# Full-row score products, normalization of attention moved behind the output product, and a new order of the fillers

## The chip, the cores and the metric

The kernel runs on one core of a Trainium2 chip. The metric is the device time of one execution in microseconds (us). TensorE is called PE in the rows, VectorE DVE, ScalarE ACT, GpSimd POOL and SyncE SP; SP issues nearly all DMAs.

## The reference

Three layers follow each other on 8 batches of 576 positions: a retention layer with 8 heads of 64, a mixture of 4 attention experts of which each token takes 2, and a layer with a rotation by sine and cosine and a mixing over positions. Cut to what matters here:

```python
# retention
scores = (1/8) * q @ k.T;  ret = scores * decay;  x = ret @ v          # [8, 576, 512]
# experts e = 0..3, head size 64
logits = x @ w_gate;  topk, w = best 2 of 4, softmax over the two
q, k, v = x @ wq[e], x @ wk[e], x @ wv[e]
s = (1/8) * q @ k.T, causal;  a = exp(s - max);  a /= a.sum() + 1e-9
out[token] += w[token, e] * (a @ v @ wo[e])                              # where e is in topk
# last layer
theta = out @ w_theta;  zr, zi = out*cos(theta), out*sin(theta)
u = out + w_tok_r @ zr + w_tok_i @ zi;  result = u + relu(u @ w_ch)
```

The division by the sum and the gate's weight w scale each row of a, so they may also be applied to the rows of a @ v.

## The kernel before

Products that need more than one pass of precision split a number into a high part h and a low part l: `split` (L91) writes h on ACT and l = x - h on DVE, and `mm3` (L86) adds three matmuls.

The first half of the program runs over 80 attention units (b, p, m): batch b, pair p of two experts (s = 0, 1), and block m of 128 query rows (64 in the last, m = 4). The loop at L535 does one unit's scores, then the transposes of the unit before, and the output product when a group of blocks is complete (groups are m = 0; 1 and 2; 3 and 4). Between these it calls `fill`, which takes pieces of other work from a list: projections of the second pair of this batch, then retention, V and the projections of the next batch. How much is taken is set by a table of costs, `COST` for the units and one number per piece, and `FO`. The program is then put in order by a scheduler for each engine, so the rows of an engine do not stand in the order of the code.

For a pair, `proj_qk` (L184) makes U, which holds for each expert the high part of q in one half of the partitions and its low part in the other half, and K. K's high part KN is copied by four DMAs on SP into both halves of KK (L200); K's low part KL stays where it is.

`at_scores` (L260) multiplies U by KK over all 128 rows (L272), so that high and low part of q meet the high part of K in one matmul, and then adds, over 64 rows only, the high part of q by KL (L275). On DVE L278 adds the causal mask and finds the row minimum of the negated scores, on ACT L283 takes the exponential and its row sum. `at_norm` (L287) then divides the gate's weight by the sum on three small DVE instructions (L292 to L294) and scales the row block, on DVE for s = 0 (L297) and on ACT for s = 1 (L299). `at_trans` (L310) transposes the block on PE (L324) and copies it to PT, on DVE for s = 0 and on ACT for s = 1 (L329, L331). `at_out` (L333) multiplies V by PT (L343), and ACT copies the result to ob (L347), which goes out to a DRAM tile OD. Scores, transposes and outputs share four PSUM tiles named a.

The second half reads OD back (`load_o`, L477, tiles ol) and makes token tiles from it (`token_tile`, L481); nine of them are made early, in the last batch of the first half. Then follow `mix` (L621) and `channel` (L671), whose result POOL completes (L684).

Of the kernel before, what the change touches and what calls it, by code (L numbers as in the profile page):

```python
# [9 lines left out]
F32 = mybir.dt.float32  # L10
# [34 lines left out]
FO = 0.5  # L45
NDVE = (0,)
# [7 lines left out]
def tile_kernel(ctx: ExitStack, tc: tile.TileContext, qk, kv, w1, wo, wot, wd, cst, out):  # L54
# [10 lines left out]
    TT = [dram.tile([128, 2, DM], F32, name=f"tt{k}") for k in range(4)]  # L65
    att = pool("att", side="right")
# [9 lines left out]
    LG = [att.tile([128, NCH, E], F32, name=f"lg{i}") for i in range(2)]  # L76
    WH = w1p.tile([128, 4, NW1], F32R, name="WH")
# [106 lines left out]
    def proj_qk(b, p, t, g):  # L184
        xh, xl = XT[b]
        if (b, p) not in QKP:
            QKP[b, p] = (att.tile([128, 2, S], F32R, name="U", bufs=2), att.tile([128, 2, S], F32R, name="KK", bufs=2),
                         att.tile([128, S], F32R, name="KL", bufs=2), att.tile([128, S], F32R, name="KN", bufs=1))
        U, KK, KL, KN = QKP[b, p]
# [5 lines left out]
        if t:  # L195
            split(KN[:, sl], KL[:, sl], ps)
            if g:
                for s in range(2):
                    for o in range(2):
                        nc.sync.dma_start(KK[o * 64:o * 64 + 64, s, :].bitcast(F32),  # L200
                                          KN[s * 64:s * 64 + 64, :].bitcast(F32))
            return
# [57 lines left out]
    def at_scores(u):  # L260
        b, p, m = u
        U, KK, KL, _ = QKP[b, p]
# [3 lines left out]
        st = att.tile([128, 4, 2], F32, name="st", bufs=3)  # L266
        parts = [(0, n)] if n <= 512 else [(0, HS), (HS, S)]
        Ps = [att.tile([128, S], F32, name="P", bufs=PB_N) for _ in range(2)]
        for i, (j0, j1) in enumerate(parts):
            ps = [ps1.tile([128, j1 - j0], F32, name="a", bufs=AB, padded_shape=[128, 512]) for _ in range(2)]  # L270
            for s in range(2):
                nc.tensor.matmul(ps[s][:R], U[:, s, rs], KK[:, s, j0:j1], start=True, stop=False)  # L272
            for s in range(2):
                hs = slice(s * 64, s * 64 + 64)
                nc.tensor.matmul(ps[s][:R], U[hs, s, rs], KL[hs, j0:j1], start=False, stop=True)  # L275
# [6 lines left out]
        for s in range(2):  # L282
            MARK["act"] = nc.scalar.activation(Ps[s][:R, :n], Ps[s][:R, :n], AF.Exp, bias=st[:R, last, s:s + 1], scale=-1.0,  # L283
                                 accum_out=st[:R, 2, s:s + 1])
        PB[u] = (Ps, st)

    def at_norm(u):  # L287
        b, p, m = u
        Ps, st = PB[u]
        R = ROWS[m]  # L290
        n = min(C * (m + 1), S)
        nc.vector.tensor_scalar(st[:R, 3, :], st[:R, 2, :], 1e-9, None, op0=OP.add)  # L292
        nc.vector.reciprocal(st[:R, 3, :], st[:R, 3, :])
        nc.vector.tensor_mul(st[:R, 3, :], GW[b][:R, m, 2 * p:2 * p + 2], st[:R, 3, :])  # L294
        for s in range(2):
            if s in NDVE:
# [494 lines left out]
```

## Time and profile before

| | us |
|---|---|
| median of 3 runs | 986.61 (985.03 to 989.39) |
| the profiled execution | 989.46 |
| span of its instructions | 987.7 |
| PE busy in the span | 958.8 |
| DVE, ACT, POOL busy | 683.4, 487.1, 226.7 |

An engine's busy time is the union of its instructions' times. Matmuls are pipelined: one starts before the one ahead has ended, so the time that a matmul costs is read from the distance between starts. A wait is idle time of an engine, put down to what ended it.

### The profile page before, as it was taken

Reading aid. Unit: us, or ns where it says so; the run is one execution under the profiler, and the core shown is the slowest. Engines: PE = TensorE matmul, PEld = TensorE weight load, DVE = VectorE, ACT = ScalarE, POOL = GpSimd, SP = SyncE. Lnnn points to the kernel's source line nnn. Section 1 sums busy time; section 2 is a strip of 40 time slices with the busy share of each in tenths; the row PEclk is TensorE's granted clock in tenths of the full one; section 3 lists DMA queues with packets and bytes.
Section 4 is the critical chain, followed back from the end, with each engine's and each line's share of the span. In section 5 each row is a group of like instructions: output and inputs, shape, how many; then the busy total and the mean of one; then the engine's idle time right before and its main releaser. Section 6 shows DMA issues by size and latency. Waiting matters only on the chain.

```text
span 987.7 us, 21586 instructions
## 1 busy us (share of the span) xinstructions
PE 958.8 (97%) x8090; PEld 848.1 (86%) x8090; DVE 683.4 (69%) x2099; ACT 487.1 (49%) x1278; POOL 226.7 (23%) x278
## 2 busy tenths in 40 slices
PE   6999999999999999999999999999999999999998
PEld 6988878778787877777767899999999999999998
DVE  5498887888978779687576783485655746486533
ACT  2366656656666565566567652344333432344320
POOL 4334262452624525332000001020200102020110
PEclk9999999999999999999999999999999999999999
DMA  9755563654635636354631301010001001010001
GB/s 267 199 166 155 154 194 89 195 172 124 212 111 171 194 106 204 98 163 132 243 127 37 121 2 48 14 60 25 36 13 37 37 1 49 1 38 12 25 26 48
DMA packets 64185, 101.45 MB, mean 103 GB/s; under 512 B 15184, under 2 KB 37072, under 8 KB 64080
## 3 DMA queue, kind: packets, MB, share of 16 engines
q1 hardware_dynamic: 63936, 99.79, 33.1%
q8 instruction: 64, 1.05, 0.4%
q0 software_dynamic: 144, 0.28, 0.1%
q14 instruction: 41, 0.34, 0.1%
HBM read 67.22 MB, written 23.66 MB: 92 GB/s over the span
## 4 chain that ended last, share of the span: by engine, by line
PE 83%; DVE 10%; DMA 3%; issue 1%; ACT 1%; SPq 1%; POOL 1%; ACTq 0%; POOLq 0%
PE acc L658 24%; PE w L87 12%; PE w L88 11%; PE w L89 11%; PE a L343 4%; PE a L324 4%; PE a L272 3%; PE a L275 2%; PE w L125 2%; PE w L157 2%; PE w L153 2%; PE acc L648 2%; DMA kv<-kv 2%; DVE P L278 2%; DVE sm L130 1%
## 5 line engine op out<-in xcount | busy, mean ns | idle before, releaser
L658 PE MATMUL acc<-TK,zh 128*128 128x256 f32 (+1 forms) x1024 | 183.8, 302 | 0.0
L658 PEld LDWEIGHTS acc<-TK,zh 128*128 128x128 f32 x1024 | 152.4, 190 | 0.7 <-DVE ul L93 0.2
L684 POOL TENSOR_TENSOR o<-o,ul 128x576 f32<-128x576 f32 x28 | 41.9, 1500 | 435.2 <-DVE o L679 435.2
L283 ACT ACTIVATE P<-P,st 128x128 f32<-128x128 f32 (+4 forms) x160 | 95.8, 599 | 69.4 <-DVE st L278 68.6
L658 PE MATMUL acc<-TK,zl 128*128 128x256 f32 (+1 forms) x512 | 110.0, 297 | 0.0
L278 DVE CUSTOM_DVE_ANT_0 P<-a,cm 128x128 f32<-128x128 f32 (+4 forms) x160 | 72.8, 476 | 26.9 <-PE a L275 26.4
L658 PEld LDWEIGHTS acc<-TK,zl 128*128 128x128 f32 x512 | 86.2, 189 | 0.1
L602 ACT ACTIVATE cs<-cs 128x512 f32<-128x512 f32 x72 | 45.2, 630 | 80.3 <-DVE cs L600 76.7
L92 ACT ACTIVATE zh<-cs 128x512 fp32r<-128x512 f32 x64 | 40.2, 630 | 81.3 <-PE acc L658 67.0
L87 PE MATMUL w<-xh,WH 128*128 128x288 f32 x256 | 79.9, 312 | 0.0
L93 DVE TENSOR_TENSOR zl<-cs,zh 128x512 fp32r<-128x512 f32 x64 | 45.0, 707 | 50.4 <-ACT zh L92 49.4
L88 PE MATMUL w<-xl,WH 128*128 128x288 f32 x256 | 76.3, 298 | 0.0
L324 PE MATMUL a<-ident,P 128*128 128x128 f32 (+2 forms) x480 | 65.2, 265 | 11.1 <-DVE P L297 5.2
L87 PE MATMUL w<-uh,CH 128*128 128x256 f32 (+1 forms) x256 | 75.8, 296 | 0.0
L89 PE MATMUL w<-uh,CH 128*128 128x256 f32 (+1 forms) x256 | 75.8, 296 | 0.0
L88 PE MATMUL w<-ul,CH 128*128 128x256 f32 (+1 forms) x256 | 75.8, 296 | 0.0
L89 PE MATMUL w<-xh,WL 128*128 128x288 f32 x256 | 75.6, 295 | 0.0
L604 DVE SCALAR_TENSOR_TENSOR cs<-cs,x 128x512 f32<-128x512 f32 x72 | 55.4, 775 | 24.6 <-ACT cs L602 24.5
L125 PE MATMUL w<-qz,kt 128*64 128x256 f32 (+1 forms) x576 | 61.8, 334 | 7.7 <-DMA kt<-qk 5.1
L167 POOL TENSOR_TENSOR xl<-xt,xh 128x512 fp32r<-128x512 f32 (+1 forms) x40 | 50.7, 1269 | 78.8 <-ACT xh L166 78.8
L324 PEld LDWEIGHTS a<-ident,P 128*128 128x128 f32 (+2 forms) x480 | 45.7, 138 | 26.1 <-DVE P L297 7.4
L93 DVE TENSOR_TENSOR ul<-acc,uh 128x256 fp32r<-128x256 f32 x64 | 25.7, 450 | 59.3 <-ACT uh L92 59.1
(141 smaller groups left out, 2484.7 us busy)
## 6 DMA issues: line engine op xcount, KB each, us to landing
kv<-kv SPq DMA_DIRECT2D x40, 512.0 KB, 4.8
KK<-KN SPq DMA_DIRECT2D x64, 144.0 KB, 2.5
raw<-wd SPq DMA_DIRECT2D x43, 192.0 KB, 2.8
qz<-qk SPq DMA_DIRECT2D x64, 128.0 KB, 4.1
kt<-qk SPq DMA_DIRECT2D x32, 256.0 KB, 3.7
out<-o SPq DMA_DIRECT2D x28, 288.0 KB, 2.1
td<-hl SPq DMA_DIRECT2D x27, 192.0 KB, 2.5
TK<-td SPq DMA_DIRECT2D x9, 576.0 KB, 8.0
```

The source lines that it names most:

```text
L87: nc.tensor.matmul(ps, ah, bh, start=first, stop=False)
L88: nc.tensor.matmul(ps, ah, bl, start=False, stop=False)
L89: nc.tensor.matmul(ps, al, bh, start=False, stop=last)
L93: nc.vector.tensor_sub(l, src, h)
L125: nc.tensor.matmul(ps[e][g, i, :, j * 64:R], t[:, hp, j * 64:j * 64 + 64], qz[:, :, hp, j * 64:R], start=True, stop=True, skip_group_check ...
L167: nc.gpsimd.tensor_sub(xl[:, :, cs], xt, xh[:, :, cs])
L278: MARK["dve"] = nc.vector.tensor_tensor_reduce(Ps[s][:R, j0:j1], ps[s][:R], cm[:R, o + j0:o + j1], 1.0, st[:R, 0, s:s + 1] if i else 3.0e3 ...
L283: MARK["act"] = nc.scalar.activation(Ps[s][:R, :n], Ps[s][:R, :n], AF.Exp, bias=st[:R, last, s:s + 1], scale=-1.0, accum_out=st[:R, 2, s:s ...
L324: nc.tensor.transpose(tp[:w, j, :], Ps[s][:R, j * C:j * C + w], ident[:R, :R])
L602: nc.scalar.activation(cs, cs, AF.Sin)
L604: nc.vector.scalar_tensor_tensor(z, cs, -1.0, x2[:, None, ds].to_broadcast([128, 2, 256]), op0=OP.mult, op1=OP.mult)
L658: nc.tensor.matmul(acc[d][j], A[:, dc], TK[:, kt, W, t0:t1], start=q == 0 and n == 0, stop=q == 8 and n == 2)
```

## The change

Both parts of K are now split into one tile KN of two parts (two buffers instead of one), and the four DMAs copy both into KK, so that the low product also runs over 128 rows with the same U; it now adds low part by low part as well. The sums of the exponentials are kept for a whole pair in SUM. `at_norm` runs once per pair: it makes the quotients for all five blocks, transposes them on DVE in squares of 32, and four DMAs write them as rows to a DRAM tile GD. `load_o` reads them back, spread over 64 partitions by four DMAs, and POOL multiplies ol by them. In the loop, part of the fillers now comes before the transposes and the rest after them; `COST` and `FO` have other numbers.

```diff
-FO = 0.5
-NDVE = (0,)
+FO = 0.45
...
+    GD = [dram.tile([2, 2, 640], F32, name=f"gd{b}") for b in range(B)]
...
+    SUM = [att.tile([128, NCH, 2], F32, name=f"sum{i}") for i in range(2)]
+    NW = [att.tile([128, 32], F32, name=f"nw{i}") for i in range(2)]
...
-            QKP[b, p] = (att.tile([128, 2, S], F32R, name="U", bufs=2), att.tile([128, 2, S], F32R, name="KK", bufs=2),
-                         att.tile([128, S], F32R, name="KL", bufs=2), att.tile([128, S], F32R, name="KN", bufs=1))
+            QKP[b, p] = (att.tile([128, 2, S], F32R, name="U", bufs=2), att.tile([128, 2, 2, S], F32R, name="KK", bufs=2),
+                         att.tile([128, 2, S], F32R, name="KN", bufs=2))
...
-            split(KN[:, sl], KL[:, sl], ps)
+            split(KN[:, 0, sl], KN[:, 1, sl], ps)
...
-                        nc.sync.dma_start(KK[o * 64:o * 64 + 64, s, :].bitcast(F32),
-                                          KN[s * 64:s * 64 + 64, :].bitcast(F32))
+                        nc.sync.dma_start(KK[o * 64:o * 64 + 64, s, :, :].bitcast(F32),
+                                          KN[s * 64:s * 64 + 64, :, :].bitcast(F32))
...
             for s in range(2):
-                nc.tensor.matmul(ps[s][:R], U[:, s, rs], KK[:, s, j0:j1], start=True, stop=False)
-            for s in range(2):
-                hs = slice(s * 64, s * 64 + 64)
-                nc.tensor.matmul(ps[s][:R], U[hs, s, rs], KL[hs, j0:j1], start=False, stop=True)
+                for x in range(2):
+                    nc.tensor.matmul(ps[s][:R], U[:, s, rs], KK[:, s, x, j0:j1], start=x == 0, stop=x == 1)
...
-                                 accum_out=st[:R, 2, s:s + 1])
+                                 accum_out=SUM[p][:R, m, s:s + 1])
...
+        x = SUM[p]
+        w = NW[p][:, :2 * NCH].rearrange("q (m s) -> q m s", m=NCH)
-        nc.vector.tensor_scalar(st[:R, 3, :], st[:R, 2, :], 1e-9, None, op0=OP.add)
-        nc.vector.reciprocal(st[:R, 3, :], st[:R, 3, :])
-        nc.vector.tensor_mul(st[:R, 3, :], GW[b][:R, m, 2 * p:2 * p + 2], st[:R, 3, :])
-        for s in range(2):
-            if s in NDVE:
-                nc.vector.tensor_scalar(Ps[s][:R, :n], Ps[s][:R, :n], st[:R, 3, s:s + 1], None, op0=OP.mult)
-            else:
-                nc.scalar.activation(Ps[s][:R, :n], Ps[s][:R, :n], AF.Copy, scale=st[:R, 3, s:s + 1])
+        nc.vector.tensor_scalar(w, x, 1e-9, None, op0=OP.add)
+        nc.vector.reciprocal(w, w)
+        nc.vector.tensor_mul(w, GW[b][:, :, 2 * p:2 * p + 2], w)
+        wt = att.tile([128, 32], F32, name="nwt", bufs=2)
+        nc.vector.transpose(wt, NW[p])
+        for a in range(4):
+            nc.sync.dma_start(GD[b][p].rearrange("s (m a q) -> a m s q", m=NCH, a=4)[a], wt[a * 32:a * 32 + 2 * NCH, :])
...
     def load_o(b):
         OL[b] = wk1.tile([128, 2, S], F32, name="ol", bufs=3)
         nc.sync.dma_start(OL[b], OD[b])
+        gw = wk1.tile([128, 2, S], F32, name="og", bufs=1)
+        for s in range(2):
+            for p in range(2):
+                nc.sync.dma_start(gw[s * 64:s * 64 + 64, p, :], GD[b][p, s, :S].partition_broadcast(64))
+        nc.gpsimd.tensor_mul(OL[b], OL[b], gw)
...
-    COST = [0.7, 1.1, 1.6, 2.2, 2.2]
+    COST = [0.9, 1.2, 1.7, 2.2, 2.4]
...
+        goal = tot * (k + 1) / 10 if t < nu else 1e9
+        fill(done + FO * max(goal - done, 0.0), k)
         if t >= 1:
             at_trans(units[t - 1])
-        goal = tot * (k + 1) / 10 if t < nu else 1e9
-        fill(goal - FO, k)
+            if units[t - 1][2] == NCH - 1:
+                at_norm(*units[t - 1][:2])
+        fill(goal, k)
         if t >= 1:
             ub, up, um = units[t - 1]
             if GROUPS[GRP[um]][-1] == um:
                 at_out(ub, up, GRP[um])
-        if t < nu:
-            at_norm(units[t])
-        fill(goal, k)
```

The scheduler makes of this another order. The first place is on PE, in the second batch, from the transposes of block 2 to the scores of block 4. P is transposed by ident (128x128), V by PT is the output product, U by KK and KL the scores, and qz, kt, sm, S and vp belong to retention; the line of dots stands for the two rows ahead of it once more. Before:

```order
L324 MATMUL a<-ident,P 128x128 x6
L153 MATMUL w<-qz_111,S_108 64x128
L157 MATMUL w<-sm_114,vp 64x128 x2
L157 MATMUL w<-sm_115,vp 64x128 x2
...
L343 MATMUL a<-PT,V 64x256 x4
L343 MATMUL a<-PT,V 64x128 x2
L272 MATMUL a<-KK,U 64x288 x2
L275 MATMUL a<-KL,U 64x288 x2
L272 MATMUL a<-KK,U 64x288 x2
L275 MATMUL a<-KL,U 64x288 x2
```

The same place on PE now, where L322 transposes, L341 makes the output and L127 belongs to retention:

```order
L322 MATMUL a<-ident,P 128x128 x6
L127 MATMUL w<-qz_122,kt 64x256 x2
L127 MATMUL w<-qz_122,kt 64x2x64
L341 MATMUL a<-PT,V 64x256 x4
L341 MATMUL a<-PT,V 64x128 x2
L275 MATMUL a<-KK,U 64x288 x8
L322 MATMUL a<-ident,P 128x128 x8
```

The four steps between high and low part are one row of eight equal matmuls, and three products instead of nine stand between the transposes and the output that reads their copies.

The second place is on PE at the border between two batches, where the first scores of the new pair (128 columns) stand among the projections of the other pair (xh, xl by WH, WL). Before:

```order
L89 MATMUL w<-xh,WL 128x288
L87 MATMUL w<-xh,WH 128x288
L272 MATMUL a<-KK,U 128x128
L275 MATMUL a<-KL,U 128x128
L272 MATMUL a<-KK,U 128x128
L275 MATMUL a<-KL,U 128x128
L324 MATMUL a<-ident,P 128x64 x4
L324 MATMUL a<-ident,P 64x64
```

The same border on PE now; the line of dots stands for 21 projections:

```order
L89 MATMUL w<-xh,WH 128x288
L90 MATMUL w<-xl,WH 128x288
L275 MATMUL a<-KK,U 128x128 x2
L91 MATMUL w<-xh,WL 128x288
L89 MATMUL w<-xh,WH 128x288
...
L89 MATMUL w<-xh,WH 128x288
L275 MATMUL a<-KK,U 128x128 x2
L322 MATMUL a<-ident,P 128x64 x4
L322 MATMUL a<-ident,P 64x64
```

The scores of the second expert have moved behind almost two more projections.

The third place is on SP, where the second half's inputs are first read back. Before:

```order
L200 DMA KK<-KN 64x576 x2
L479 DMA ol<-od_60 128x1152
L479 DMA ol<-od_61 128x1152
L479 DMA ol<-od_62 128x1152
L349 DMA od_67<-ob 128x576
L479 DMA ol<-od_63 128x1152
```

The same place on SP now; gd are the quotients, og their spread copy, nwt the transposed quotients:

```order
L479 DMA ol<-od_60 128x1152
L483 DMA og<-gd_85 64x576 x4
L479 DMA ol<-od_61 128x1152
L297 DMA gd_92<-nwt 5x2x32 x3
L483 DMA og<-gd_86 64x576 x4
L297 DMA gd_92<-nwt 5x2x32
L347 DMA od_67<-ob 128x576
```

Each read of ol is followed by four reads of quotients, and the quotients of the last batch are written between them.

## Rows read from the trace of the kernel before

**Rows 1.** The page's first part: busy us (share of the span) and instructions

```profile
PE 958.8 (97%) x8090; PEld 848.1 (86%) x8090; DVE 683.4 (69%) x2099; ACT 487.1 (49%) x1278; POOL 226.7 (23%) x278
```

**Rows 2.** Stretches: length, busy PE, PEld, DVE, ACT, POOL, clock, DMA, GB/s

```profile
40.00:560.00 520.00, 504.15 (x4755) 413.35 (x4754) 411.87 (x1482) 322.52 (x947) 166.73 (x221) 0.99 0.50 152
120.00:160.00 40.00, 38.60 (x418) 31.72 (x414) 32.05 (x115) 24.36 (x75) 17.77 (x22) 0.96 0.54 164
200.00:240.00 40.00, 38.47 (x347) 33.36 (x345) 30.83 (x109) 23.71 (x77) 16.86 (x24) 0.96 0.46 128
320.00:360.00 40.00, 37.85 (x369) 32.77 (x367) 30.28 (x118) 24.73 (x79) 19.03 (x25) 0.96 0.50 149
```

**Rows 3.** Waits of PE: us in total, times, the longest one

```profile
PE a L324 <- DVE P L297: 5.2, 7, 1.4
PE a L324 <- DVE st L278: 2.9, 4, 1.3
PE a L324 <- ACT ob L347: 2.8, 2, 1.5
PE w L87 <- ACT oh L92: 1.3, 1, 1.3
```

**Rows 4.** Timeline of PE, scores of 256 columns: start, us, then the instruction

```profile
204.31 0.50 PE L272 MATMUL a<-KK,U 128*128 128x256 f32 x2
204.74 0.38 PE L275 MATMUL a<-KL,U 64*128 64x256 f32 x2
205.06 0.33 PE L324 MATMUL a<-ident,P 128*128 128x128 f32 x1
```

**Rows 5.** Timeline of PE, scores of 384 columns

```profile
213.24 0.52 PE L272 MATMUL a<-KK,U 128*128 128x384 f32 x2
213.69 0.45 PE L275 MATMUL a<-KL,U 64*128 64x384 f32 x2
214.06 0.33 PE L324 MATMUL a<-ident,P 128*128 128x128 f32 x1
```

**Rows 6.** Timeline of PE, scores of twice 288 columns, the first half

```profile
225.29 0.29 PE L89 MATMUL w<-xh,WL 128*128 128x288 f32 x1
225.42 0.43 PE L272 MATMUL a<-KK,U 128*64 128x288 f32 x2
225.78 0.35 PE L275 MATMUL a<-KL,U 64*64 64x288 f32 x2
226.06 0.34 PE L272 MATMUL a<-KK,U 128*64 128x288 f32 x1
```

**Rows 7.** Timeline of PE, scores of 128 columns at a batch border

```profile
231.43 0.22 PE L272 MATMUL a<-KK,U 128*128 128x128 f32 x1
231.58 0.32 PE L275 MATMUL a<-KL,U 64*128 64x128 f32 x1
231.84 0.33 PE L272 MATMUL a<-KK,U 128*128 128x128 f32 x1
```

**Rows 8.** Timeline, eight transposes and the copy of the second four on ACT

```profile
227.24 1.03 PE L324 MATMUL a<-ident,P 128*128 128x128 f32 x8
...
229.28 0.57 ACT L329 COPY PT<-a 128x512 f32<-128x512 f32 x1
```

**Rows 9.** Groups by line: instructions, then busy us, mean ns, idle before

```profile
L299 ACT ACTIVATE P<-P,st 128x128 f32<-128x128 f32 (+4 forms) x80 | 48.3, 604 | 15.5 <-DVE st L294 14.3
...
L684 POOL TENSOR_TENSOR o<-o,ul 128x576 f32<-128x576 f32 x28 | 41.9, 1500 | 435.2 <-DVE o L679 435.2
L297 DVE TENSOR_SCALAR P<-P,st 128x128 f32<-128x128 f32 (+4 forms) x80 | 40.8, 510 | 1.5
...
L294 DVE TENSOR_TENSOR st<-gw,st 128x2 f32<-128x2 f32 (+1 forms) x80 | 18.1, 226 | 0.8
```

**Rows 10.** DMAs of KK (the page's sixth part) and of ol (time to landing)

```profile
KK<-KN SPq DMA_DIRECT2D x64, 144.0 KB, 2.5
...
DMA to landing us min/median/max: 3.4/4.4/6.4
```

More of the change, by code (lines that the diff above doesn't have):

```diff
@@ L186, in proj_qk @@
         if (b, p) not in QKP:
-            QKP[b, p] = (att.tile([128, 2, S], F32R, name="U", bufs=2), att.tile([128, 2, S], F32R, name="KK", bufs=2),
-                         att.tile([128, S], F32R, name="KL", bufs=2), att.tile([128, S], F32R, name="KN", bufs=1))
-        U, KK, KL, KN = QKP[b, p]
+            QKP[b, p] = (att.tile([128, 2, S], F32R, name="U", bufs=2), att.tile([128, 2, 2, S], F32R, name="KK", bufs=2),
+                         att.tile([128, 2, S], F32R, name="KN", bufs=2))
+        U, KK, KN = QKP[b, p]
         w0 = (2 * p + t) * 128
@@ L261, in at_scores @@
         b, p, m = u
-        U, KK, KL, _ = QKP[b, p]
+        U, KK, _ = QKP[b, p]
         R = ROWS[m]
@@ L265, in at_scores @@
         rs = slice(m * C, m * C + R)
-        st = att.tile([128, 4, 2], F32, name="st", bufs=3)
+        st = att.tile([128, 2, 2], F32, name="st", bufs=3)
         parts = [(0, n)] if n <= 512 else [(0, HS), (HS, S)]
@@ L283, in at_scores, with at_norm @@
             MARK["act"] = nc.scalar.activation(Ps[s][:R, :n], Ps[s][:R, :n], AF.Exp, bias=st[:R, last, s:s + 1], scale=-1.0,
-                                 accum_out=st[:R, 2, s:s + 1])
[L285 to L291, printed above, removed]
-        nc.vector.tensor_scalar(st[:R, 3, :], st[:R, 2, :], 1e-9, None, op0=OP.add)
-        nc.vector.reciprocal(st[:R, 3, :], st[:R, 3, :])
-        nc.vector.tensor_mul(st[:R, 3, :], GW[b][:R, m, 2 * p:2 * p + 2], st[:R, 3, :])
-        for s in range(2):
-            if s in NDVE:
-                nc.vector.tensor_scalar(Ps[s][:R, :n], Ps[s][:R, :n], st[:R, 3, s:s + 1], None, op0=OP.mult)
-            else:
-                nc.scalar.activation(Ps[s][:R, :n], Ps[s][:R, :n], AF.Copy, scale=st[:R, 3, s:s + 1])
+                                 accum_out=SUM[p][:R, m, s:s + 1])
+        PB[u] = Ps
+    def at_norm(b, p):
+        x = SUM[p]
[7 more added lines that the diff above has]
+            nc.sync.dma_start(GD[b][p].rearrange("s (m a q) -> a m s q", m=NCH, a=4)[a], wt[a * 32:a * 32 + 2 * NCH, :])
     def pt_view(PT, g, j):
@@ L311, in at_trans @@
         b, p, m = u
-        Ps, _ = PB.pop(u)
+        Ps = PB.pop(u)
         R = ROWS[m]
@@ L366, in tile_kernel @@
         nc.gpsimd.memset(l, 0.0)
+    for x in SUM + NW:
+        nc.gpsimd.memset(x, 1.0)
     loads(0, 0)
```

## The prediction

> **What bounds the kernel now.** Read the busy line first [rows 1]: PE is busy for 958.8 of 987.7 us, DVE for 683.4, ACT for 487.1. So only two things can move the time: work that leaves or joins TensorE's own stream, and the moments in which that stream stands still. Then cut the span into stretches [rows 2]. In 40 to 560 us, where attention, retention and projections run, PE is busy for 504.15 of 520 us, so it idles 15.9 us, while DVE is busy for 79% and ACT for 62% of it. Three stretches of 40 us have a mean granted clock of 0.96, which is a mixture of the two levels 2.4 and 1.2 GHz; each loses 0.04 x 40 = 1.6 us, and in each PE had idled for 1.4 to 2.2 us. All that the change does to the order lies before 560 us; behind that it adds only work for POOL and the DMA queues.
>
> The table of waits says who holds PE up [rows 3]: transposes that wait for the normalization on DVE (5.2 us), for the row minima (2.9) and for a PSUM tile that ACT still copies from (2.8), and a token tile that waits for the split of its input (1.3). Last come the single matmuls around a score [rows 4 to 7]. L272 is the full-row product with K's high part, L275 the 64-row product with its low part. What I read there is not how long one takes but how far its start lies from the next start.
>
> **Term 1, the scores on PE.** The number of matmuls stays (192 + 192 become 384), only their rows change. A full-row matmul of 288 columns is followed by the next after 225.42 - 225.29 = 0.13 us [rows 6]; in proportion to columns I estimate 0.12 for 256, 0.175 for 384 and 0.235 for 512. For 128 columns the same rule gives 0.06; the eight transposes of 128 columns took 1.03 us, 0.13 each at most and 0.11 if the last one's tail is taken off [rows 8]. I take 0.11 and keep 0.06 and 0.13 as ends.
> At 384 columns, two L272 occupy 0.45 us up to the first L275, and the two L275 0.37 up to the next instruction [rows 5]. Four full rows would take 4 x 0.175 = 0.70, so 0.12 goes. The first pair alone should take 0.35; the 0.10 more is the price of entering the 64-row products. The pair of L275 takes no less than two full ones (0.37 against 0.35), though both share a time slot. At 288 columns it is 0.36 and 0.28 = 0.64 against 0.52 [rows 6]: 0.12, twice in a unit of the last rows. At 256 columns 0.75 [rows 4], of which some 0.09 is the entry from the 64-column products ahead, which stays: against 0.48 + 0.09 it is 0.18. At 512 I estimate 0.10 + 0.47 + 0.43 against 0.94: 0.06. At 128 columns one single L272 with its L275 takes 231.84 - 231.43 = 0.41 [rows 7] against 2 x 0.11: 0.19. Eight of the sixteen units of 128 columns are cut in this way, s by s, as in the second place of the section on the change, and save 0.38 each; the other eight save an estimated 0.14.
> Sum: (0.12 + 0.24 + 0.18 + 0.06) x 16 = 9.6, and 8 x 0.38 + 8 x 0.14 = 4.2: 13.8 us, with the ends of the 128-column spacing 12.5 to 16.2. The order has about as many changes between 128- and 64-column products as before, so these cancel. Term 1: -14.
> Here a page of the Trainium skill speaks against the change. Both matmuls of an L275 pair lie on different row halves, and the rows show that the pair takes 0.28 us at 288 columns [rows 6], where two in a row at 0.13 would take 0.26 without any entry or exit. The Trainium skill, "TensorE: Matmul & The Clock Gate", Part 3 (packing small matmuls), says that matmuls on different row groups run concurrently, so that packing them gains. By that rule, unpacking adds one streaming per pair; the rows bear it out for the pair but show more lost at its edges, so the sum goes by the rows.
>
> **Term 2, the normalization leaves the units.** Per unit three small DVE instructions (the last 226 ns), one scaling on DVE (510 ns) and one on ACT (604 ns) go; 80 of each, 40.8 us on DVE and 48.3 on ACT for the scalings, 18.1 for one of the three small ones [rows 9]. In their place come, once per pair, three small ones and a transpose, 64 instead of 400. None of that was PE's work, so it counts only by PE's waits. The wait for L297 (5.2) has no cause any more. Of the two others (2.9 and 2.8), I take half, since minima and output copies remain while DVE and ACT have less in front of them: -2.9. Together -8. With the waits, two of the three stretches at 0.96 should return to full clock: 2 x 1.6 = -3.2. The ends: nothing of this, or all 15.9 us of idling and 4.8 of clock.
>
> **What it adds.** (a) K's parts: a pair's four DMAs carry twice the bytes, and the first waits for DVE's low part as well as ACT's high part. The row has 2.5 us to landing for the present size [rows 10]; more bytes lie between 2.5 and 5. At the eight batch borders the order now puts the second head's 128-column score behind two more projections' worth of work, some 3 us, so the later landing is covered; if not, each border costs up to 1 us. I take 1 us in all, ends 0 and 8. (b) The output product now stands closer behind its transposes. By the order, 19 of 48 outputs have less than 1.3 us of PE's work after their last transpose, 6 before. The copies in between are on DVE and ACT: in the rows ACT's copy began 1.0 us and ended 1.6 us after the eight transposes [rows 8], because exponentials stood ahead of it. In the new order half of the fillers lie between score and transpose, so ACT should be through with them. I take 0.1 us at each of the 19 places, 2 us. (c) 64 small DMAs on SP for the quotients, in groups of four that wait for the transpose on DVE; behind them stand loads that are needed much later, so nothing. (d) In the second half eight POOL products of 1152 columns: from 1500 ns for 576 columns [rows 9] 3.0 us each, plus 32 DMAs of the size of a KK transfer. POOL is nearly empty there. Only the first token tile can feel it: its input lands after 4.4 us [rows 10] and PE already waits 1.3 us for it; now four more DMAs and 3 us of POOL come on top. But the order has moved that tile two scores later, some 4 us of PE's work. I take 0.5 us, ends -1.3 and +5.
> Sum: -14 - 8 - 3.2 + 1 + 2 + 0.5 = -21.7. From the profiled execution's own 989.46 us that is 967.8. This execution was 2.85 us above the median of 986.61, as I guess by waits or slow-clock stretches of the kind that I remove, so part of the gain is already in the median: between 964.9 and 967.8 I forecast 967.
>
> **The rivals.** (B) Only PE's own stream gets shorter: the waits that go are replaced by others of the same size. For it: each of them is a single wait below 2 us, and every reordering makes new ones. Against: DVE's work in that stretch falls from 411.87 us by 40.8, by some 50 for the small ones, and gains some 15, which leaves about 68% of a shorter stretch. 986.6 - 14 + 1 = 974. (C) The pairs' concurrency was worth what the page says and their edges cost nothing that leaves: then each pair of batch and head pair adds 0.06 + 0.12 + 0.175 + 0.235 + 2 x 0.13 = 0.85 us, 16 times 13.6, against 9 from the waits: 991. Against it stand the 0.45 and 0.37 [rows 5]. (D), on the other side: outputs wait for late copies. If ACT's copy still ends 1.6 us behind the transposes, 19 outputs wait up to 1.2 us each, 23 us, and half a dozen more stretches fall to 0.96 for 1.6 us each, 10: 986.6 - 14 - 8 + 33 = 998. It decides against the gain as soon as the mean wait at those places passes 1 us. For it: the copy row. Against: the exponentials now end earlier, and DVE's copies are prompt. (E) The first token tile waits for its weighted input: 5 us and a stretch of slow clock, 974.
>
> **How the numbers follow.** Forecast 0.70 (own range 958 to 977), B 0.12, C 0.05, D 0.08, E 0.05. The lowest end is -16.2 - 15.9 - 4.8 with nothing added, about 951; the highest within the forecast's mechanism is -12.5 with 13 of additions, about 986. The range that leaves out two in ten is 954 to 984. Within 0.5%, 981.7 to 991.5, a measurement of this kernel can't tell from no change. Faster by more takes nearly all of the forecast and E and most of B: 0.84; within it are most of C and rests of B and D: 0.08; slower: 0.08.
>
> **What would show it.** Right: scores whose starts follow each other at 0.12 to 0.24 us with no step before the second half of a pair; PE busy for some 490 us before a boundary that lies near 540; no wait for a scaled P; no or one stretch at 0.96. Wrong: output products at PE's head that wait for PT copies (D), scores that wait for KK's landing, a token tile that waits for POOL (E), or score groups that last longer than now (C).

## The result, and the profile after

The changed kernel takes 998.7 us (median of 4 runs, 994.8 to 1002.0), the kernel before in the same comparison 985.8 (984.7 to 989.4). The ratio is 1.0122, with a 95% interval of 1.009 to 1.0154: slower by 1.2%, clear of the noise, where 967 us were forecast with a range of 954 to 984.

The busy line of the page after, beside [rows 1]: PE is busy for 6 us less and the span has grown by 12.

```profile
PE 952.8 (95%) x8090; PEld 863.1 (86%) x8090; DVE 647.5 (65%) x1843; ACT 445.7 (45%) x1198; POOL 244.5 (24%) x290
```

The stretches of after, columns as in [rows 2], with one more from the end of the first half:

```profile
40.00:560.00 520.00, 487.64 (x4699) 418.48 (x4698) 360.54 (x1207) 275.02 (x854) 172.26 (x225) 0.97 0.60 172
...
200.00:240.00 40.00, 35.02 (x293) 31.58 (x287) 23.13 (x79) 17.84 (x60) 14.65 (x20) 0.87 0.48 134
520.00:560.00 40.00, 34.16 (x179) 25.43 (x179) 22.81 (x57) 19.69 (x49) 8.51 (x4) 0.96 0.40 118
```

ACT is emptier as worked out (275.0 us instead of 322.5) and DVE less so (360.5 instead of 411.9, where the prediction's sum for rival B comes to some 336). And yet PE stands still for 32 of 520 us instead of 16. The mean clock of the stretch has gone from 0.99 to 0.97, that of 200 to 240 us from 0.96 to 0.87.

The waits of PE after. No row of [rows 3] is left among the large ones; the first is new, and as large as all the waits on DVE before:

```profile
PE a L341 <- DVE PT L327: 14.9, 13, 3.6
PE w L127 <- DMA kt<-qk: 7.0, 4, 2.8
PE pS L89 <- DVE nr L513: 3.5, 2, 2.3
PE a L341 <- ACT PT L327: 3.0, 3, 1.4
PE w L89 <- DVE nr L513: 2.8, 3, 2.1
PE a L275 <- DMA KK<-KN: 2.5, 2, 1.3
PE acc L663 <- DVE zl L95: 1.8, 1, 1.8
```

L341 is the output product and L327 the copy of the transposed P (PT) out of PSUM: output products wait 17.9 us, at 16 places, for PT copies. The L127 row, retention's load, was there before (5.1 us).

To compare kernels I cut each span of a trace into three: **idle** (between PE's first and last instruction neither PE nor its weight loads run), **clock** (half of the time in which 1.2 GHz instead of 2.4 were granted, that is the span times one minus the mean granted clock) and the rest, PE's **stream**, which includes some 5 us ahead of PE's first instruction and behind its last.

| us | span | idle | clock | stream |
|---|---|---|---|---|
| before | 987.7 | 23.6 | 8.5 | 955.6 |
| after | 1000.0 | 41.8 | 18.8 | 939.5 |
| difference | +12.3 | +18.2 | +10.3 | -16.1 |

So the gain that was forecast in the stream came, and more than all of it was handed back in waits and in the slow clock that follows them. The table has one execution of each kernel, and that of after is the slowest of four. Over all executions with a recorded clock the clock's part is 9.9 to 19.0 us in after (median 14.0, n = 4) and 2.9 to 12.9 before (median 5.9, n = 25): the difference is nearer to 8 us than to 10.3, and the clock column of a single trace is uncertain by several us.

**What the late copy waits for.** The longest wait of after, 3.60 us, as a timeline of PE, DVE and POOL:

```profile
206.50 3.24 PE L341 MATMUL a<-PT,V 128*64 128x192 f32 x20 [3.60 <-DVE PT L327]
...
202.84 0.26 DVE L410 TENSOR_SCALAR ex<-raw 128x192 int32<-128x192 int32 x1 [2.05 <-POOL r L416]
203.02 0.74 DVE L408 SCALAR_TENSOR_TENSOR b<-raw,b 128x192 int32<-128x192 int32 x1
203.80 1.30 DVE L412 SCALAR_TENSOR_TENSOR b<-ex,b 128x192 f32<-128x192 int32 x1
...
205.42 0.69 DVE L166 TENSOR_TENSOR xt<-w,gt 128x512 f32<-128x512 f32 x1
206.03 0.41 DVE L327 COPY PT<-a 128x256 f32<-128x256 f32 x1
...
201.21 1.04 POOL L113 TENSOR_TENSOR vp<-kv,gam 128x512 f32<-128x512 f32 x1 [2.23 <-DMA kv<-kv]
202.21 0.59 POOL L416 TENSOR_TENSOR r<-r,ex 128x192 f32<-128x192 f32 x1
```

The transposes were through at 202.2. The PT copy (L327) began at 206.03, since in the trace DVE runs in the order of its queue, and ahead of the copy stood a weight conversion (L407 to L413, the jobs that the loop spreads over the first half) and retention's product xt (L166). Its second step waited 2.05 us for POOL, which held the only buffer ex and had itself waited 2.23 us for retention's kv. In the trace of before 4 of DVE's 112 PT copies have a conversion instruction between the last score reduction and themselves, 4 instructions in all; in after 48 copies have 145. The product xt stands between a last reduction and its copy 42 times in after and never before.

Conversions are late for their own loads too. In the trace of before neither DVE nor ACT has a wait for loaded words (raw); after:

```profile
ACT r L415 <- DMA raw<-wd: 13.6, 10, 3.4
DVE b L407 <- DMA raw<-wd: 11.8, 8, 2.6
```

From the issue of such a load on SP to the moment when DVE is free for it pass 12.1 us before (median of 51) and 5.9 after. A possible reason stands in SP's own queue (the fourth round tests it), where L297 is now the store of the quotients (64 pieces of 1.2 KB; ns min/median/max):

```profile
L297 SPq DMA_DIRECT2D gd<-nwt x64: 686/732/1270, 78.4 to 552.1; - x64
```

Each takes SP 0.73 us to issue, longer than a load of words (L400, most of them 192 KB: median 0.43 in after, 0.34 before). The lengths of all of SP's DMA issues between 40 and 490 us sum to 169 us before and to 238 after; of the 69 more, these stores are 39 and the doubled key parts 13.

### The profile page after: what moved, and what is told of

It reads as the page before. It is cut to its first block, busy times and chain, and to the rows that moved or that the text cites. A ratio compares the mean times of both kernels' runs of the same rounds, so it can differ in the third digit from the quotient of the medians.

```text
span 1000.0 us, 21417 instructions
## 1 busy us (share of the span) xinstructions
PE 952.8 (95%) x8090; PEld 863.1 (86%) x8090; DVE 647.5 (65%) x1843; ACT 445.7 (45%) x1198; POOL 244.5 (24%) x290
## 4 chain that ended last, share of the span: by engine, by line
PE 74%; DVE 9%; DMA 6%; ACT 2%; issue 2%; SPq 1%; POOL 0%; DVEq 0%; ACTq 0%; POOLq 0%
PE acc L663 23%; PE w L89 9%; PE w L90 9%; PE w L91 9%; PE a L341 5%; PE a L275 5%; PE w L127 3%; PE a L322 3%; DMA raw<-wd 3%; PE acc L653 2%; PE w L159 2%; DMA KK<-KN 1%; DVE P L278 1%; PE w L155 1%; DVE b L412 1%
## 5 line engine op out<-in xcount | busy, mean ns | idle before, releaser
L275 PE MATMUL a<-KK,U 128*64 128x288 f32 (+4 forms) x384 | 81.0, 335 | 4.6 <-DMA KK<-KN 2.5
L341 PE MATMUL a<-PT,V 128*64 128x192 f32 (+3 forms) x576 | 66.6, 351 | 18.1 <-DVE PT L327 14.9
L89 PE MATMUL w<-xh,WH 128*128 128x288 f32 x256 | 77.7, 304 | 0.0
L341 PEld LDWEIGHTS a<-PT,V 128*64 128x64 f32 (+1 forms) x576 | 41.7, 147 | 39.9 <-DVE PT L327 17.7
L609 DVE SCALAR_TENSOR_TENSOR cs<-cs,x 128x512 f32<-128x512 f32 x72 | 59.7, 835 | 24.6 <-ACT cs L607 24.5
L275 PEld LDWEIGHTS a<-KK,U 128*128 128x128 f32 (+1 forms) x384 | 57.1, 178 | 17.1 <-issue 5.6
L169 POOL TENSOR_TENSOR xl<-xt,xh 128x512 fp32r<-128x512 f32 (+1 forms) x40 | 47.1, 1178 | 86.7 <-ACT xh L168 85.5
```

The lines of the kernel that those rows point to most:

```text
L89: nc.tensor.matmul(ps, ah, bh, start=first, stop=False)
L169: nc.gpsimd.tensor_sub(xl[:, :, cs], xt, xh[:, :, cs])
L275: nc.tensor.matmul(ps[s][:R], U[:, s, rs], KK[:, s, x, j0:j1], start=x == 0, stop=x == 1)
L341: nc.tensor.matmul(po[s * 64:s * 64 + 64, c0:], V[:ROWS[j], j, 2 * p + s, :], v, start=j == 0, stop=j == last, skip_group_check=True)
L609: nc.vector.scalar_tensor_tensor(z, cs, -1.0, x2[:, None, ds].to_broadcast([128, 2, 256]), op0=OP.mult, op1=OP.mult)
```

## The experiments

**First round: the parts one at a time.** Rows alone put the four full-row matmuls of a score into the kernel before; normalization alone moved only that; order alone took only the loop, FO and COST; and the last kept all of the change but gave it the old loop, FO and COST.

```diff
 # order alone; e4 is the reverse of it on the changed kernel
-FO = 0.5
+FO = 0.45
-    COST = [0.7, 1.1, 1.6, 2.2, 2.2]
+    COST = [0.9, 1.2, 1.7, 2.2, 2.4]
+        fill(done + FO * max(goal - done, 0.0), k)
         at_trans(units[t - 1])
-        fill(goal - FO, k)
+        fill(goal, k)
         at_out(ub, up, GRP[um])
...
```

> The kernel before with the full-row scores alone (both parts of K in KK, larger KK transfers); normalization and loop order as before. Theory 1 (the new order of transposes, fillers and outputs costs the time): the score stream is 13 to 16 us shorter and little of it is lost to waits, so 0.983 to 0.988 of before. Theory 2 (more and larger DMAs on SP delay the conversion's loads, and DVE stands behind them): part of it is lost again, 0.990 to 1.000. Theory 3 (PE's time is given by waits that any shorter stream refills): 0.995 to 1.005.

> The kernel before with the normalization moved to the second half alone (quotients transposed on DVE, written by small DMAs, read back and multiplied on POOL); scores and loop order as before. Theory 1: the waits for the scaled P go, 5 us, so 0.990 to 0.998, less up to 4 us where POOL's products hold DVE up. Theory 2: the 64 small DMAs on SP delay the loads behind them, PT copies wait on DVE, 1.000 to 1.010. Theory 3: 0.995 to 1.005.

> The kernel before with the new loop order and cost table alone (part of the fillers before the transposes, the normalization of each unit after the output). Theory 1: output products wait for PT copies as in the changed kernel, 1.010 to 1.030. Theory 2: without the added DMAs the copies come in time, 0.995 to 1.005. Theory 3: 0.995 to 1.005.

> The changed kernel with the loop order and cost table of before: full-row scores and the moved normalization, transposes directly behind the scores, then fillers, then the output. Theory 1: both gains show, 0.975 to 0.985. Theory 2: as slow as the changed kernel, 1.005 to 1.015. Theory 3: 0.995 to 1.005.

| | ratio (95%) | idle | clock | stream |
|---|---|---|---|---|
| e1, rows alone | 1.0029 (1.0004 to 1.0055) | 32.2 | 8.5 | 946.5 |
| e2, normalization alone | 1.0019 (0.9999 to 1.0039) | 27.1 | 8.5 | 947.9 |
| e3, order alone | 1.0213 (1.0179 to 1.0248) | 35.7 | 17.9 | 951.7 |
| e4, all but the order | 1.0015 (0.9983 to 1.0047) | 37.0 | 10.2 | 938.4 |

The loss is the order's: alone it costs 2.1%, and under it rows and normalization together gain 0.9%. (Theory 1 fits e3, theory 3 fits e1 and e4, and e2 lies where theories 2 and 3 overlap.) The first wait of e3 is the one of after:

```profile
PE a L343 <- DVE PT L329: 15.0, 8, 3.3
```

Yet no engine waits for loaded words in e3. In the longest of these waits (3.31 us, up to 146.05) DVE worked all the time: from 142.40 us on, when a wait for POOL had ended, it ran a conversion, the three small instructions of the normalization, a scaling of P and xt ahead of the copy. So the new order loses time at the copies also where every load is in time.

But the order is not the whole story. In e1 and e4 the stream is 9 and 17 us shorter and the time is not. In e1 (first fence) the waits of [rows 3] have grown to fill it; in e4 (second) the copies of outputs on ACT (ob) and PT copies are late:

```profile
PE a L322 <- DVE P L295: 8.4, 14, 1.9
PE a L322 <- ACT ob L345: 7.2, 5, 3.0
```

```profile
PE a L322 <- ACT ob L345: 10.3, 6, 2.5
PE a L341 <- DVE PT L327: 6.4, 7, 2.0
...
ACT r L415 <- DMA raw<-wd: 13.2, 8, 3.4
DVE b L407 <- DMA raw<-wd: 12.1, 9, 2.6
```

**Second round: what stands ahead of the copies.**

```diff
 # e5: a job is issued behind the latest PT copy of its engine
+            MARK["dve" if s in PTV else "act"] = copy(PT[...], tp[...])
 # e6, e7: more buffers for the conversions
-raw bufs=2, b1/ex/r/d bufs=1, hl bufs=2
+raw bufs=4, b1/ex/r/d bufs=2, hl bufs=3
 # e8
-FO = 0.45
+FO = 0.0
```

> The changed kernel with one thing moved: each conversion job is issued behind the latest PT copy of DVE and of ACT instead of behind the latest reduction and exponential of a score, which takes conversion instructions out of the way of many PT copies (in the trace of the changed kernel 48 of DVE's 112 copies have 145 conversion instructions between the last score reduction and themselves; of the kernel before 4 have 4). Theory 1 (head of line: outputs wait because the in-order queues of DVE and ACT hold a conversion job, itself late for its load or for POOL, ahead of a PT copy): TensorE's waits for PT copies fall from 18 us to 7 or less, the slow-clock loss from 15 to 9, so the ratio to the kernel before comes to 0.995 (0.988 to 1.002). Theory 2 (distance: outputs stand too close behind the transposes, whatever is ahead in the queues): the waits for PT copies stay at 15 or more and the ratio at 1.012 (1.008 to 1.016).

> The changed kernel with more buffers for the conversions (4 instead of 2 for the loaded words, 2 instead of 1 for each intermediate, 3 instead of 2 for the result), the order of the scores, transposes and outputs nearly as before. Theory 1 (head of line, and the job is late because its load is): DVE's and ACT's waits for the loaded words, 11.8 and 13.6 us, fall below 5 each, TensorE's waits for PT copies from 18 to 11, the ratio from 1.012 to 1.003 (0.996 to 1.008). Theory 2 (distance): the waits for loaded words fall, but those for PT copies stay at 15 or more, ratio 1.012. If the loads come no earlier with more buffers because SP's queue holds them, both numbers stay.

> Full-row scores and the moved normalization under the old order, with more buffers for the conversions (as in the run beside it). Under the old order without them the ratio was 1.0015, with 12.1 and 13.2 us of waits on DVE and ACT for the loaded words and 28 us of TensorE's idling. Theory 1 (late conversion jobs hold copies up): idling falls to 20 us, slow clock to 8.5, ratio 0.991 (0.984 to 0.997). Theory 2 (the copies themselves and their distance): the waits for loaded words go but the ratio stays at 1.001 (0.998 to 1.005).

> The changed kernel with the share of fillers between a score and the transposes of the unit before it set from 0.45 to 0, so that all of them stand between transposes and output; the cost table is the new one. Theory 2 (distance) says: TensorE's waits for PT copies fall from 18 to some 7 us, as under the old order, and transposes that wait for exponentials or for a PSUM tile take 6 to 10 in their place; ratio 1.002 (0.997 to 1.006), the same as the old order (1.0015). Theory 1 (head of line) expects the same sign, since the order by instructions has 13 copies with 13 conversion instructions ahead instead of 48 with 145; it differs in the run that moves the jobs and not the transposes.

Measured: e5 1.0039 (0.9999 to 1.0078), with 23 copies and 69 conversion instructions left instead of 48 and 145 (and xt still ahead of 42 copies); e6 0.9997 (0.9969 to 1.0025); e7 1.0007 (0.9976 to 1.0038); e8 1.0047 (1.0015 to 1.0078). e5 moves only the jobs and wins back two thirds of the loss, e6 only their buffers and wins back all of it. That the conversion jobs cost the time is thus shown; that they do so at the head of the queue alone is not. e5 lies between the two theories with both its numbers: PT waits fell to 12.5 us, where theory 1 said 7 or less and theory 2 said 15 or more, and its ratio is above the one range and below the other. In e6 they fall to 13.1, and 49 copies still have 178 conversion instructions ahead, but DVE's and ACT's waits for words are down from 25.4 us to 5.2. What falls more is the clock loss, in the traces from 18.8 to 10.2 (e5) and 6.8 (e6), over all executions from a median of 14.0 to 9.9 and 9.8. The waits of e5:

```profile
PE a L341 <- DVE PT L327: 11.9, 12, 3.0
...
PE a L341 <- ACT PT L327: 0.6, 1, 0.6
```

e8 agrees with distance as well: with all fillers behind the transposes the PT waits fall to 1.2 us, but waits for ob copies come to 12.6 in their place (2.8 before). e7 missed. Under the old order more buffers don't help: the median time from a load's issue to DVE's being free for it grows from 5.8 us (e4) to 15.7, but at 7 of 51 jobs it is still below 3.5 us (10 in e4), and DVE waits 12.2 us for words and ACT 8.9. The expectation of e9 has it that the loads stood where they had stood; that holds for these few jobs alone.

**Third round: the loads themselves.** Each conversion's words are loaded one job earlier.

```diff
         def job(k):
+            load(*spec[k + 1][1:])          # words of the next job; raw bufs=3
-            nc.sync.dma_start(raw, src...)
             ...
 # e12 only
-        nc.gpsimd.tensor_mul(OL[b], OL[b], gw)
+        nc.vector.tensor_mul(OL[b], OL[b], gw)
```

> Full-row scores and moved normalization under the old order, and each conversion's words are loaded one job (some 8 us) before the job that uses them; three buffers for them instead of two. With more buffers alone, the loads stood where they had stood in SP's queue, right ahead of their job, and DVE still waited 12.2 us for them; the ratio stayed at 1.0007. Theory 1 (conversion jobs that wait for their load hold ob and PT copies up): DVE's and ACT's waits for the loaded words fall below 3 us each, TensorE's waits for ob copies from 10 to 12 us to 5, idling between 30 and 550 us from 28 to 20, ratio 0.988 (0.982 to 0.994). Theory 2 (the copies are late for other reasons, exponentials and the copies themselves): the waits for the words go, the ratio stays at 1.001 (0.998 to 1.004).

> The changed kernel with each conversion's words loaded one job earlier and three buffers for them; the order of DVE and ACT as in the changed kernel. Theory 1: what made the conversions late is gone, though they still stand ahead of 48 PT copies: TensorE's waits for PT copies fall from 18 to 11, ratio 0.999 (0.993 to 1.005), as with more buffers (0.9997). Theory 2 (distance): 1.012.

> Control: the kernel before with each conversion's words loaded one job earlier. In its trace DVE waits 0.2 us and ACT not at all for these words, so all theories expect no change: ratio 1.000 (0.997 to 1.003). If it is below 0.995, the earlier load helps by something else than the wait.

> As e9, and the four products of the outputs with the quotients, 1152 columns each, are made on DVE instead of POOL. In the traces with the product on POOL TensorE waits 4 to 8 us for nr and zl on DVE between 510 and 560 us, and single DVE instructions beside the product last 2.7 us instead of 0.4. Theory C (POOL's product slows DVE's instructions down): these waits fall to some 2 us, as in the kernel before, and the run is 2 to 4 us (0.2 to 0.4%) below e9. Against it: DVE gets four products of some 1.2 to 2.5 us each, which may hold the same tiles up; then the two are equal.

Measured: e9 0.9909 (0.9874 to 0.9945), e10 0.9963 (0.9936 to 0.999), e11, the control, 1.0004 (0.9974 to 1.0034), e12 0.9887 (0.985 to 0.9924). The early load does nothing where the words were never waited for, and gives 1.6% to the changed kernel and 1.1% to its old-order form. That late words cost the changed kernel more than it lost is thus shown by the time. Its trace doesn't show the whole way: between the transposes' end and a late PT copy DVE is idle for words only twice (1.15 and 2.02 us). Under the old order the way is not shown: the waits of DVE and ACT for words are 25.3 us in e4, 21.1 in e7, which gains nothing, 14.5 in e9 and 19.5 in e12, which is the fastest of the four. The waits of e9, where the 18.7 us of waits for ob and PT in e4 became 13.3:

```profile
PE a L322 <- ACT ob L345: 6.2, 5, 2.1
PE a L275 <- ACT ob L345: 4.0, 5, 1.0
...
PE a L341 <- DVE PT L327: 2.7, 3, 1.8
```

Two parts of the expectation failed in e9: DVE still waits 10.9 us for words, at 4 places instead of 9, and PE's waits for ob copies are 10.2 us (11.3 in e4), where 5 were expected. e12 lies 0.2% below e9, as expected, but the intervals overlap. Its trace has the reason at least: in after, POOL's product with the quotients stretched a DVE instruction beside it.

```profile
525.93 2.67 POOL L484 TENSOR_TENSOR ol<-ol,og 128x1152 f32<-128x1152 f32 x1 [5.44 <-DMA gd<-nwt]
...
526.15 2.72 DVE L511 TENSOR_SCALAR k<-k 128x512 f32<-128x512 f32 x1
```

That instruction lasts 0.42 us elsewhere; here it ended 0.27 us after POOL's. The waits for zl, 1.8 us in e9, are gone in e12.

**Fourth round: the stores, and which part earns the gain.**

```diff
 # e13: kernel before, plus the four stores (nothing reads them)
 # e14, e16, e18: one store for a pair, rows picked out by the reads
-        for a in range(4):
-            nc.sync.dma_start(GD[b][p].rearrange(...)[a], wt[a * 32:a * 32 + 2 * NCH, :])
+        nc.sync.dma_start(GD[b][p], wt)
 # e15, e17: rows alone and normalization alone, words loaded early
 # e16, e18: early words, one store, product on DVE; old and new order
```

> The kernel before, and at the end of each head pair a small DVE copy and four stores of 1.2 KB on SP, as the changed kernel makes them for its quotients; nothing reads them. Theory S (SP's queue: these stores take 39 us of SP's issuing time and push the loads behind them back): the lead of a conversion's load, from its issue to DVE's coming to it, falls from 12 us to 10 or less, but it stays above what the landing takes (about 3 us) in nearly all jobs, since DVE is no earlier; ratio 1.002 (0.999 to 1.006). Theory E (the loads are late only because DVE and ACT, relieved of the scalings, come to them earlier): the lead stays at 12, ratio 1.000 (0.998 to 1.003).

> The changed kernel, and a pair's transposed quotients go out in one store of 16 KB instead of four of 1.2 KB; the reads in the second half pick the rows out, in 160 DMAs instead of 32. Theory S: SP issues 48 DMAs fewer in the first half, some 30 us less; the lead of the conversions' loads rises from 5.9 to 8 or more, DVE's and ACT's waits for them fall from 25 us to 12 or less, ratio 1.006 (1.000 to 1.010). Theory E: lead and waits as in the changed kernel, ratio 1.012 (1.008 to 1.016). A mishap that either would share: the finer reads hold the first token tile up, which would show as waits for oh between 505 and 560 us.

> The kernel before with full-row scores alone and each conversion's words loaded one job earlier. Without the earlier load the ratio was 1.0029, though TensorE's stream was 9 us shorter; its waits had grown by 9 us (for the scaled P, for ob copies, for minima), and the waits for loaded words were only 1.6 us. If late loads are what eats the gain of the rows too: 0.994 (0.990 to 0.998). If it is DVE's and ACT's own fullness (DVE is busy for 81% of the stretch and ACT for more than in the changed kernel), the early load does nothing: 1.002 (0.999 to 1.006). I hold the second the likelier.

> Old order, full-row scores, moved normalization, conversions loaded one job earlier, products on DVE, and one store for a pair's quotients. Without the last item the ratio was 0.9887. Theory S expects 3 us more off: 0.985 (0.981 to 0.989). Theory E expects no change: 0.989 (0.985 to 0.992); the finer reads may cost a little before the second half.

> The kernel before with the moved normalization alone and each conversion's words loaded one job earlier; scores as before, half of them in 64 rows. Joint theory (the rows' shorter stream pays only when DVE and ACT are relieved too, and the relief alone only removes waits): 0.997 (0.993 to 1.000), the waits for loaded words, 8.9 and 5.6 us without the early load, below 4 in all. Theory of the normalization alone (the rows are worth nothing at all, the relief everything): 0.991 (0.988 to 0.995), as with both. By the stream of TensorE, which was 8 us shorter than before with the normalization alone and 17 with both, I hold the joint one the likelier.

> The changed kernel in its own order with all mends: words loaded one job earlier, one store per pair, products on DVE. Under the old order the same came to 0.9852. If the order costs only through the late jobs ahead of the copies, the two should meet: 0.986 (0.982 to 0.990). If outputs so close behind their transposes cost by themselves, as 10 us of waits for PT copies with the early load suggest: 0.992 (0.988 to 0.996), with 8 to 12 us of waits for PT copies left. I hold the second the likelier.

| | ratio (95%) | idle | clock | stream | lead of the loads |
|---|---|---|---|---|---|
| e13 before, small stores | 1.0039 (1.0014 to 1.0065) | 25.4 | 8.5 | 957.2 | 11.8 |
| e14 after, one store | 1.0081 (1.0044 to 1.0118) | 39.2 | 14.1 | 940.4 | 6.7 |
| e15 rows, early load | 1.0006 (0.998 to 1.0033) | 28.1 | 11.3 | 946.4 | 16.4 |
| e17 normalization, early load | 0.995 (0.9926 to 0.9974) | 23.6 | 7.6 | 948.4 | 18.5 |
| e16 combined, old order | 0.9852 (0.9812 to 0.9893) | 27.4 | 8.5 | 933.3 | 15.0 |
| e18 combined, new order | 1.0059 (1.0034 to 1.0085) | 36.9 | 11.9 | 939.6 | 15.0 |

(The lead is the median time from a load's issue to DVE's being free for it.) The small stores, with one small DVE copy per pair, cost the kernel before 0.4% though nobody reads them, but not by the way of theory S: the lead stays at 11.8, and it is the waits for P and ob that grow, as far as one trace tells. In e14 the lead rises by only 0.8 us, so theory S's size for it failed; the waits for words fell from 25.4 to 12.9 us, and its ratio and the 1.0122 overlap. What shortens the lead is thus mostly the two parts themselves: 8.0 us with rows alone (e1), 10.9 with normalization alone (e2), 5.8 with both (e4).

e15 and e17 divide the gain. Rows alone earn nothing measurable even with early words. The 9 us come back as waits for DVE and ACT, which still carry the scalings, and as slow clock; the waits of e15:

```profile
PE a L322 <- DVE P L295: 7.3, 10, 1.5
...
PE a L322 <- ACT ob L345: 4.7, 4, 1.5
PE a L322 <- DVE st L276: 4.6, 8, 0.9
```

Normalization with early words earns 0.5%, both 0.9% (e9): the intervals of e17 and e9 overlap, so that the rows add something on top is likely, by a stream that is 12 us shorter, and not shown.

e16, 973.3 us, beats both kernels. Its 0.9852 is what theory S expects, but the intervals of e16 and e12 (0.9887) overlap, so that the single store earns anything is not shown. e18 missed: with the same mends the new order came out above e10 and not below. Its first half ends where that of e10 does (the first mixing matmul at 541.7 us in both), with the words in time and PT waits still there:

```profile
PE a L340 <- DVE PT L326: 9.8, 12, 1.9
...
PE w L89 <- ACT uh L94: 4.3, 1, 4.3
PE acc L676 <- ACT zh L94: 3.2, 1, 3.2
```

So a wait of about 10 us belongs to the new order with every word in time. It need not come from closeness by itself, since 49 copies still have 178 conversion instructions and 42 have xt ahead of them. The longest of these waits, with DVE busy throughout:

```profile
202.09 0.71 PE L340 MATMUL a<-PT,V 128*64 128x192 f32 x6 [1.87 <-DVE PT L326]
...
198.83 1.20 DVE L407 TENSOR_SCALAR ex<-raw 128x192 int32<-128x192 int32 x1
...
200.73 0.26 DVE L410 TENSOR_SCALAR ex<-b 128x192 int32<-128x192 int32 x1
201.02 0.69 DVE L166 TENSOR_TENSOR xt<-w,gt 128x512 f32<-128x512 f32 x1
201.63 0.41 DVE L326 COPY PT<-a 128x256 f32<-128x256 f32 x1
```

No run has early words and the jobs and xt behind the copies under the new order, so how the 10 us divide stays open. From 541.7 us on, e18's trace takes 9.3 us more than that of e10, of which 5.1 are slow clock (none in e10) and 2.2 idle time. The reason that its trace shows is my mend: the finer reads are twenty per batch, and SP issued one batch's in a row for 14 us. DVE's product waited 9.3 us for reads at the head of its queue (first fence SP's timeline, second DVE's waits), and PE's wait for uh, which ended at 585.45, comes behind the longest of these, which ended at 580.71; the wait for zh ended at 541.68, just before that boundary. In e16 the same reads held DVE up for only 0.3 us, so they cost by where they fall.

```profile
505.48 14.00 SPq L495 DMA_DIRECT2D og<-gd  x20
```

```profile
DVE ol L497 <- DMA og<-gd: 9.3, 4, 3.7
```

## Why the prediction was wrong

**Term 1 (scores on PE, -14) was right in kind and too large.** The timeline of PE after, scores of 256, 384, 288, 512 and 128 columns, to set beside [rows 4 to 7]:

```profile
308.38 0.73 PE L275 MATMUL a<-KK,U 128*128 128x256 f32 x4
308.95 0.30 PE L89 MATMUL w<-xh,WH 128*128 128x288 f32 x1
...
151.22 0.97 PE L275 MATMUL a<-KK,U 128*128 128x384 f32 x4
152.02 0.28 PE L89 MATMUL w<-WH,xh 128*128 128x260 f32 x1
...
162.86 1.27 PE L275 MATMUL a<-KK,U 128*64 128x288 f32 x8
163.97 0.30 PE L89 MATMUL w<-xh,WH 128*128 128x288 f32 x1
...
156.77 1.09 PE L275 MATMUL a<-KK,U 128*128 128x512 f32 x4
157.70 0.30 PE L89 MATMUL w<-xh,WH 128*128 128x288 f32 x1
...
238.94 0.33 PE L275 MATMUL a<-KK,U 128*128 128x128 f32 x2
239.20 0.82 PE L322 MATMUL a<-ident,P 64*128 64x64 f32 x10
```

From the start of a score to the next instruction pass 0.57 us at 256 columns (0.75 before), 0.80 at 384 (0.82), 0.93 at 512 (0.94 forecast), 1.11 for all eight at 288 (two times 0.64 before) and 0.26 at 128 (0.41). 384 was put at 0.70, and behind a 128-column matmul that is right (median of eight in e1: 0.70). But in after these scores stand behind 64-column outputs, and there the entry, 0.10, which I had priced only at 256 columns, is paid as well. At 512 the row shown is the better half: where a 64-column product of retention follows, the score takes 1.10 us (1.09 before) and nothing is gained. The stream shrank by 9.1 us with the rows alone, and by 16.1 in the whole change. Normalization alone (e2) took 7.7 off it too, though it takes no matmul away; the prediction has no term for that, and no run shows why.

**Term 2 (waits -8, clock -3.2) failed.** The waits for the scaled P went, as said. But a stall that goes is a gain only if what is next is not late, and I took DVE's lower share for proof that it would not be. A share says nothing of what stands ahead of a copy in its engine's queue. Idle time grew by 18.2 us instead of falling by 8, and the clock took 10.3 in the traces, 8 by the medians of all executions, instead of giving 3.2.

**Addition (b), outputs closer behind their transposes, +2, is the step that failed by most.** I counted the 19 places and gave each 0.1 us; 16 outputs waited 1.1 us on average, 17.9 in all. I had counted PE's work between transposes and output and not the instructions between reduction and PT copy on DVE, where conversions had come to stand (48 copies instead of 4) and xt with them (42 instead of none).

**Addition (c), "nothing" for 64 small stores,** failed too: the same stores, with a small DVE copy per pair, cost the kernel before 0.4% (e13), some 4 us. I had asked only what waits behind them, not how long SP needs for each (0.73 us). By which way they cost it stays open, since the lead of the loads did not fall in e13.

**Addition (a),** +1 for the key parts, was nearly right: PE waits 2.5 us for KK, 0.3 before. The larger parts land later, after 4.2 us in e1 where [rows 10] had 2.5:

```profile
KK<-KN SPq DMA_DIRECT2D x64, 288.0 KB, 4.2
```

**Addition (d)** was put at 0.5 for the first token tile; the tile was not late, but waits for nr and zl of 8.1 us (2.0 before) stand near POOL's products.

**Rival D (late copies, 998, chance 0.08) is what happened,** with the size: it named 23 us of waits and 10 of clock, and measured are 17.9 and 10.3. Its reason was another: it had exponentials ahead of ACT's copies, and it was conversions and xt, mostly on DVE. That its 998 lies so close to the measured 998.7 is in part luck. B (974) named the exchange of waits without seeing that the new ones could be larger. C, the concurrency of row pairs, is excluded by the shorter stream of e1, and E did not occur.

## What to carry to other kernels

Before you credit a shorter stream or a stall that goes, list for each copy that the bounding engine needs what the new order puts ahead of it in its engine's queue, and for these instructions the lead of their loads; a low busy share doesn't answer that. Work that has no hurry, such as a weight conversion, belongs behind such copies and wants its data a job early: here moving the jobs alone took the loss from 1.2% to 0.4%, and the early load alone turned it into 0.4% of gain, with the old order 0.9%. Count small DMAs by the time that their queue takes to issue them and not by bytes.

## What the hardware showed unexpectedly

- A store of 1.2 KB in pieces held SP for 0.73 us (median of 64), a load of words, mostly 192 KB, for 0.43, and twenty reads of 16 to 32 KB in a row for 14.00 us.
- A DVE instruction on 512 columns took 2.72 us instead of 0.42 while POOL multiplied 1152 columns beside it, and ended 0.27 us after that product. The Trainium skill, "SBUF — State Buffer", section "SBUF: two separate sides", says that the two engines share a port pair, "an exclusive lock, not a bandwidth split", which a DVE instruction takes in a two-port mode or, against a POOL instruction that reads SBUF, with two inputs in SBUF. The row agrees: the DVE instruction stood until POOL was through (that k<-k runs in such a mode no run shows). So do others beside the same eight products: cs<-cs,x, with two inputs in SBUF, took 2.66 and 2.93 us instead of 0.69, while nr<-k,w, which reads PSUM, kept its 0.69.
- One idle time costs twice. In the stretch from 200 to 240 us of after PE idled 5 us in all, and the mean clock was 0.87. The slow level was granted from 205.2 to 215.4, of which 1.3 us lie in the wait itself, so it cost another (10.2 - 1.3) / 2 = 4.5. In before the clock fell four times between 130 and 410 us, each time behind a single PE wait of 0.94 to 1.53 us.
